# A long convolution and a two-matmul network: token tiles cut as groups of the last transform step, the first batch's last step put beside the network, and one engine for each first-step PSUM bank

## The chip, the cores and the metric

The kernel runs on one core of a Trainium2 chip. The metric is the device time of one execution in microseconds, as the median of several executions. A one-core program shows its executions within about 0.2% of each other here. The runs called fast lie within 1.5% of the fastest of the same kernel, and only such runs are compared, except for one single look that is marked.

Five units matter. **PE** is TensorE's matrix array and **PEld** its weight loads, **DVE** is VectorE, **ACT** is ScalarE, and **POOL** is GpSimd. DMA transfers are issued from a sixth queue.

## The reference, cut to what matters

```python
def _attn_ref(x, v, pos_emb, w1, w2):           # x, v: (4, 12480, 128)
    h_filt = (np.maximum(pos_emb @ w1, 0.0) @ w2) * np.exp(-0.01 * pos)[:, None]
    u = x * v
    y = irfft(rfft(u, n=2*S, axis=1) * rfft(h_filt, n=2*S, axis=0)[None], n=2*S, axis=1)[:, :S]
    return x * y

def _moe_ref(x, w_in, w_out):                   # x: (49920, 128), w_in 128x2048, w_out 2048x128
    h = x @ w_in
    return (h * np.cos(h)) @ w_out
```

The first part is a causal convolution along 12480 positions, for 4 batches of 128 channels. The second part is a network applied to each of the 49920 tokens. Everything is fp32.

## The kernel before

The convolution is a Fourier transform split as 96 by 120, so that each of its steps is a set of matmuls with small tables. There are four steps per batch: the **first step** (`f1`), the **middle step** with the product with the filter's spectrum (`f2`), the **third step** (`i1`) and the **last step** (`i2`). Between them the data lies in one SBUF array, `slots`. The last step works in 30 groups. A group yields 4 × 104 output rows of 128 channels, and needs four rows of tables (`tm`).

The network works on tiles of tokens, in 16 steps a tile. A step is: an up matmul into a hidden PSUM bank `ph`, ACT's `a`, DVE's `k`, GpSimd's `f` (range reduction), ACT's sine `cs`, DVE's gate `gt`, and a down matmul that adds to the accumulator `acc`:

```python
TOK = 4 * N2                                    # 480 tokens a tile, 26 tiles a batch
ps_acc = tile_pool(name="ps_acc", bufs=1, space=PSUM)    # accumulator
ps_h   = tile_pool(name="ps_h",  bufs=4, space=PSUM)     # hidden ring, also for transposes
ps_c   = tile_pool(name="ps_c",  bufs=3, space=PSUM)     # banks "cv" of the transforms
# one pass of the loop is one step:
    hidden[i] = moe_up(mpool, n, c)                       # PE up, ACT a, DVE k, POOL f
    gates[i - 1] = moe_act(mpool, *hidden.pop(i - 1))     # ACT cs, DVE gt
    if i >= LAG:                                          # LAG = 4
        pn, pc = steps[i - LAG]
        moe_down(pn, pc, gates.pop(i - LAG))              # PE down
        if pc == NFC - 1:
            ots[pn] = moe_evict(mpool, pn)                # ACT copies acc to ot
    ...                                                   # transposes of the next and last tile
    owed += 1.0
    while owed > 0.0:
        owed -= next(conv, owed)                          # a piece of a transform
```

The generator `conv` yields pieces of the transforms of later batches, each with a weight in network steps. Before, only the transforms of batches 1 to 3 ran beside the network. Batch 0 was finished first, with its last step as a stage of its own:

```python
with tc.tile_pool(name="spare", bufs=2) as pool:
    for _ in i2_units(bank, 0, 3, lambda t, n2: make_third(pool, t, n2, bank)):
        pass
...
def convolutions():
    here = NT * NFC - 3 * NFC
    less = here / (CONV_STEPS + H // UA * U_STEPS)
    for steps in u_units(1, 4, slots[0:R, :, :, :], nc.vector):   # load x and v of batch 1
        yield steps * less
    for b in range(1, B):
        for steps in conv_units(bank, b):       # b == 1 makes all table rows once more, stores them
            yield steps * (less if b == 1 else 1.0)
        ready = b
```

A first-step bank was emptied by two engines in turn, as the filter's version shows (the data's version has one copy on ACT and two instructions on DVE):

```python
def f1_evict_filter(ps, b):
    ...
    nc.scalar.copy(out=fnear[0:ODD, :, :, b, :], in_=near[0:ODD])
    nc.vector.tensor_copy(out=fnear[ODD:KE, 0, :, b, :], in_=near[ODD:KE, 1])
    nc.scalar.copy(out=ffar[0:ODD, :, :, b, :], in_=far[0:ODD])
    nc.scalar.copy(out=ffar[ODD:KE, 0, :, b, :], in_=far[ODD:KE, 1])
    yield
    nc.vector.tensor_scalar(out=fnear[ODD:KE, 1, :, b, :], in0=near[ODD:KE, 0], scalar1=-1.0, ...)
    nc.scalar.activation(ffar[ODD:KE, 1, :, b, :], far[ODD:KE, 0], AF.Copy, scale=-1.0)
    yield
```

Of the kernel before, what the change touches and what calls it, by code (L numbers as in the profile page):

```python
# [16 lines left out]
P = 128  # L17
# [13 lines left out]
def kernel(  # L31
# [43 lines left out]

    nc = tc.nc
# [23 lines left out]
    TOK = 4 * N2  # L100
# [7 lines left out]
    zd = dram.tile([B, R, N2, D], F32, name="zd")  # L108
# [3 lines left out]
    woutd = dram.tile([P, NFC, D], F32, name="woutd")  # L112
# [11 lines left out]
    def to_float32(pool, dst, raw):  # L124
# [21 lines left out]
        nc.gpsimd.tensor_tensor(low[:, :], high[:, :], power[:, :].bitcast(F32), op=ALU.mult)  # L146
        nc.sync.dma_start(dst, low[:, :])
# [3 lines left out]
    weights = []  # L151
    for c in range(0, DFF, WCOL):
        weights.append((wind[:, c:c + WCOL], in_words[:, c:c + WCOL, :]))
    for c in range(0, NFC, WCOL // D):
        weights.append((woutd[:, c:c + WCOL // D, :],
                        out_words[:, c:c + WCOL // D, :, :]))
# [13 lines left out]
    class Tables:  # L170
        def __init__(self, pool):
            self.pool = pool
            self.prod, self.moved, self.turned = (
                pool.tile([P, P], F32, name=name) for name in ("prod", "moved", "turned"))
# [8 lines left out]
        def sines(self, row, column, turn, outs, eighths=None):  # L183
# [4 lines left out]
            nc.vector.tensor_scalar(out=base, in0=row[0:p, 0:n],  # L188
                                    scalar1=column[0:p, 0:1], scalar2=None, op0=ALU.mult)
            if eighths is not None:  # L190
                nc.vector.tensor_scalar(out=base[:, eighths], in0=base[:, eighths],
                                        scalar1=float(turn // 8), scalar2=None, op0=ALU.add)
            for dst, quarters in outs:
# [3 lines left out]
                nc.vector.tensor_scalar(out=m, in0=base, scalar1=quarters,  # L197
                                        scalar2=None, op0=ALU.add)

                nc.vector.tensor_scalar(out=t, in0=m, scalar1=1.0 / turn, scalar2=ROUND,  # L200
                                        op0=ALU.mult, op1=ALU.add)
                nc.vector.tensor_scalar(out=t, in0=t, scalar1=ROUND, scalar2=float(turn),
                                        op0=ALU.subtract, op1=ALU.mult)
                nc.vector.tensor_tensor(t, m, t, op=ALU.subtract)
                nc.scalar.activation(dst, t, AF.Sin, scale=TWO_PI / turn)

    def forward_tables(pool):
        t = Tables(pool)
# [22 lines left out]
    def inverse_tables(pool):  # L231
        t = Tables(pool)
# [40 lines left out]

    def make_third(pool, t, n2, half=None):

        if n2 % 3 < 2:
            make_t(t, n2, half=half)
        else:
            spare = pool.tile([N1, 2, R], F32, name="spare")
            make_t(t, n2, spare=spare[:, :, :])  # L280
# [103 lines left out]
    def f1_evict_filter(ps, b):  # L384
        pj = ps[:, 0:4 * N1].rearrange("p (i r k) -> p r k i", i=2, r=2)
        near, far = pj[:, :, 0:KF], pj[:, :, KF:N1]
        nc.scalar.copy(out=fnear[0:ODD, :, :, b, :], in_=near[0:ODD])
        nc.vector.tensor_copy(out=fnear[ODD:KE, 0, :, b, :], in_=near[ODD:KE, 1])
        nc.scalar.copy(out=ffar[0:ODD, :, :, b, :], in_=far[0:ODD])
        nc.scalar.copy(out=ffar[ODD:KE, 0, :, b, :], in_=far[ODD:KE, 1])  # L390
        yield
        nc.vector.tensor_scalar(out=fnear[ODD:KE, 1, :, b, :], in0=near[ODD:KE, 0],
                                scalar1=-1.0, scalar2=None, op0=ALU.mult)
        nc.scalar.activation(ffar[ODD:KE, 1, :, b, :], far[ODD:KE, 0], AF.Copy, scale=-1.0)
        yield

    def f1_evict(ps, b):
        pj = ps[:, 0:4 * N1].rearrange("p (i r k) -> p r k i", i=2, r=2)
        nc.scalar.copy(out=parts[0:ODD, :, :, b, :], in_=pj[0:ODD])
        nc.vector.tensor_copy(out=parts[ODD:KE, 0, :, b, :], in_=pj[ODD:KE, 1])  # L400
        yield
        nc.vector.tensor_scalar(out=parts[ODD:KE, 1, :, b, :], in0=pj[ODD:KE, 0],
                                scalar1=-1.0, scalar2=None, op0=ALU.mult)
        yield
# [51 lines left out]
    def i2_out(pool, ps, xs, b, g):  # L456
# [4 lines left out]
        for h in range(2):  # L461
            n2 = n2s(g)[h * UA]
# [152 lines left out]
    def conv_units(bank, b):  # L615
# [12 lines left out]
        for _ in keep:  # L628
            pass
# [272 lines left out]
```

## Time and profile before

| | before |
|---|---|
| median of the runs, us | 4011.0 (4009.4 to 4016.2) |
| span of the profiled run, us | 4013.5 |
| filter's first step, us | 94 to 200 |
| batch 0: first, middle, third step, us | 200–288, 288–393, 393–464 |
| batch 0's last step, alone, us | 464–548 |
| network's first matmul, us | 550 |
| nothing but the network from, us | 3001 |

The forty slices of the kernel before, of PE's busy time and of the clock that was granted to it, in tenths, 100 us to a digit:

```profile
PE   5879878999999999999999999999999999999999
PEclk7579998999999999999999999999999999999999
```

From the eighth slice on PE is at 90% or more. What can be gained lies in the first seven slices, or in PE's own work. The **loss** of a stretch is its length less the time that its matmul records need at the record spacing seen where PE runs dense: 402.5 ns for a network record of 480 columns, 162.7 for the first step, 217 for the middle step, 102.5 for the third, 111 for the last, about 100 for a transpose. Edges of stretches are whole microseconds, so a sum over three batches is good to about 3 us. No matmul record of the network or of the mixed transforms is missing from the traces of before (6656 of the network), so none counts as loss by mistake.

Two more lines of before are needed later. They are groups from DVE's groups by shape in the load stretch 550 to 688 us: product of x and v, and `k`. Columns are busy time, mean ns of one, and idle time before them:

```profile
L368 DVE TENSOR_TENSOR xt<-xt,vt 104x256 f32<-104x256 f32 x60 | 59.7, 1011 | 0.0
L673 DVE TENSOR_SCALAR k<-a 128x480 f32<-128x480 f32 x56 | 23.0, 411 | 12.0 <-ACT a L670 11.9
```

The product takes 59.7 of the 131 us that DVE is busy there.

### The profile page before, as it was taken

To read this page: it belongs to the slowest core of one execution; us is meant where nothing else is said; L and a number is where in the kernel's file an instruction comes from. 1 tells how busy PE (TensorE), PEld (TensorE's weight loads), DVE (VectorE), ACT (ScalarE), POOL (GpSimd) and SP (SyncE) were. 2 spreads that over 40 slices of the span, in tenths; PEclk is the share of its full clock that TensorE was granted. 3 is DMA by queue.
4 is the path that set the end of the run, shared out by engine and by line. 5 is a ranking of instruction groups with operands and counts; after the bars stand their busy time and mean duration, and the time that the engine had idled before them with its cause. 6 is when DMAs were issued, how large, how long until landed. Compare 5 with 4: busy or idle time off the path is not lost.

```text
span 4013.5 us, 49256 instructions
## 1 busy us (share of the span) xinstructions
PE 3811.5 (95%) x13882; PEld 2227.9 (56%) x13882; DVE 2870.6 (72%) x6111; ACT 2589.5 (65%) x4905; POOL 2654.6 (66%) x2490
## 2 busy tenths in 40 slices
PE   5879878999999999999999999999999999999999
PEld 4666743655565655555656565556664444444444
DVE  3368669988887877887668777876556666666666
ACT  3544545866675566666655576665547777777777
POOL 6136657788865655887456658884447777777776
PEclk7579998999999999999999999999999999999999
DMA  4015353123216601221046202220350000000000
GB/s 131 26 49 175 93 140 86 53 81 85 70 49 178 190 24 35 78 74 49 11 138 173 82 26 63 78 69 15 86 159 19 20 20 20 15 20 20 20 15 15
DMA packets 285244, 276.12 MB, mean 69 GB/s; under 512 B 17389, under 2 KB 247885, under 8 KB 284717
## 3 DMA queue, kind: packets, MB, share of 16 engines
q1 hardware_dynamic: 284973, 272.99, 24.5%
q8 instruction: 111, 1.82, 0.2%
q14 instruction: 160, 1.31, 0.1%
HBM read 192.61 MB, written 80.31 MB: 68 GB/s over the span
## 4 chain that ended last, share of the span: by engine, by line
PE 75%; POOL 5%; DVE 3%; ACT 2%; DMA 2%; issue 2%; SPq 0%; POOLq 0%; DVEq 0%; ACTq 0%
PE ph L667 30%; PE acc L691 24%; PE cv L691 6%; PE cv L453 4%; PE cv L428 4%; POOL f L676 3%; PE cv L380 3%; PE cv L410 3%; PE ph L121 2%; ACT cs L681 1%; DVE k L673 1%; DMA zd<-zs 1%; DVE xt L368 1%; POOL slots L423 1%; DVE gt L683 1%
## 5 line engine op out<-in xcount | busy, mean ns | idle before, releaser
L676 POOL TENSOR_TENSOR f<-a,k 128x480 f32<-128x480 f32 x1664 | 2006.0, 1206 | 1030.2 <-DVE k L673 1001.7
L667 PE MATMUL ph<-at,w_in_sb 128*128 128x480 f32 x3328 | 1627.7, 571 | 21.0 <-DVE gt L683 20.1
L670 ACT ACTIVATE a<-ph,quarter 128x480 f32<-128x480 f32 x1664 | 1100.0, 661 | 711.4 <-PE ph L667 663.8
L683 DVE TENSOR_TENSOR gt<-ph,cs 128x480 f32<-128x480 f32 x1664 | 1092.2, 656 | 349.2 <-ACT cs L681 333.2
L691 PE MATMUL acc<-gt,w_out_sb 128*128 128x480 f32 x2720 | 1326.1, 569 | 8.7 <-ACT ot L696 8.1
L681 ACT ACTIVATE cs<-f 128x480 f32<-128x480 f32 x1664 | 998.8, 600 | 403.6 <-POOL f L676 401.5
L673 DVE TENSOR_SCALAR k<-a 128x480 f32<-128x480 f32 x1664 | 798.4, 480 | 548.1 <-ACT a L670 531.4
L691 PEld LDWEIGHTS acc<-gt,w_out_sb 128*128 128x128 f32 x2720 | 515.0, 190 | 603.6 <-issue 567.2
L667 PEld LDWEIGHTS ph<-at,w_in_sb 128*128 128x128 f32 x3328 | 593.6, 191 | 384.3 <-issue 286.0
L423 POOL TENSOR_TENSOR slots<-slots,t 120x256 f32<-120x256 f32 x384 | 307.2, 806 | 72.2 <-PE ps L410 36.8
L691 PE MATMUL cv<-gt,w_out_sb 128*128 128x480 f32 x608 | 294.2, 566 | 0.5 <-DVE gt L683 0.5
L453 PEld LDWEIGHTS cv<-slots,tm 96*104 96x104 f32 x1440 | 178.8, 169 | 78.1 <-issue 66.9
L428 PEld LDWEIGHTS cv<-cs,slots 120*96 120x96 f32 x1536 | 178.2, 167 | 71.5 <-issue 62.1
L453 PE MATMUL cv<-slots,tm 96*104 96x128 f32 x1440 | 189.2, 273 | 11.6 <-DMA tm<-td 7.9
L428 PE MATMUL cv<-cs,slots 120*96 120x120 f32 x1536 | 186.2, 267 | 6.0 <-POOL slots L423 6.0
L691 PEld LDWEIGHTS cv<-gt,w_out_sb 128*128 128x128 f32 x608 | 115.4, 190 | 130.3 <-issue 128.3
L380 PEld LDWEIGHTS cv<-c,slots 104*124 104x124 f32 x768 | 135.0, 195 | 82.9 <-issue 58.3
L410 PE MATMUL cv<-slots,w 124*120 124x256 f32 x576 | 173.3, 381 | 5.2 <-DMA h<-hd 4.6
L380 PE MATMUL cv<-c,slots 104*124 104x192 f32 x768 | 156.7, 331 | 17.3 <-POOL slots L356 15.3
L410 PEld LDWEIGHTS cv<-slots,w 124*120 124x120 f32 x576 | 103.2, 184 | 115.7 <-issue 102.7
L438 DVE TENSOR_TENSOR slots<-cv,other 96x240 f32<-96x240 f32 x384 | 136.3, 394 | 4.3 <-ACT other L436 4.3
L374 POOL TENSOR_TENSOR slots<-xt 104x256 f32<-104x256 f32 x120 | 117.4, 978 | 31.8 <-PE ph L667 17.8
(116 smaller groups left out, 2940.0 us busy)
## 6 DMA issues: line engine op xcount, KB each, us to landing
h<-hd SPq DMA_DIRECT2D x144, 240.0 KB
tm<-td SPq DMA_DIRECT2D x90, 312.0 KB
xt<-in_x_dram SPq DMA_DIRECT2D x120, 208.0 KB
vt<-in_v_dram SPq DMA_DIRECT2D x120, 208.0 KB
xs<-in_x_dram SPq DMA_DIRECT2D x120, 208.0 KB
zd<-zs SPq DMA_DIRECT2D x240, 104.0 KB
zb<-zd SPq DMA_DIRECT2D x104, 240.0 KB
out_dram<-ob SPq DMA_DIRECT2D x104, 240.0 KB
```

The costliest lines, as they stand in the source:

```text
L380: nc.tensor.matmul(ps[0:KE, i * 2 * N1:(i + 1) * 2 * N1], u[:, b, 0:KE, i], c1[0:u.shape[0], :, :].rearrange("p r k -> p (r k)"), start=Tr ...
L410: nc.tensor.matmul(ps[0:N2, i * 2 * D:(i + 1) * 2 * D], w[:, i, :], src[0:KE], start=True, stop=True)
L423: nc.gpsimd.tensor_tensor(y[:, r], y[:, r], t[:, r], op=op)
L428: nc.tensor.matmul(ps[0:N1, (i * 2 + r) * N2:(i * 2 + r + 1) * N2], parts[0:N2, r, :, b, i], cs[:, r, :], start=True, stop=True)
L453: nc.tensor.matmul(ps[0:R, i * D:(i + 1) * D], t[:, i, r, :], slots[0:N1, :, place, :], start=(r == 0), stop=(r == 1))
L667: nc.tensor.matmul(ph[:, 0:TOK], w_in_sb[:, c * P:(c + 1) * P], ats[n][:, :], start=True, stop=True)
L670: nc.scalar.activation(a[:, :], ph[:, 0:TOK], AF.Identity, bias=quarter[:, 0:1], scale=INV_TWO_PI)
L673: nc.vector.tensor_scalar(out=k[:, :], in0=a[:, :], scalar1=ROUND, scalar2=ROUND, op0=ALU.add, op1=ALU.subtract)
L676: nc.gpsimd.tensor_tensor(f[:, :], a[:, :], k[:, :], op=ALU.subtract)
L681: nc.scalar.activation(cs[:, :], f[:, :], AF.Sin, scale=TWO_PI)
L683: nc.vector.tensor_tensor(gt[:, :], ph[:, 0:TOK], cs[:, :], op=ALU.mult)
L691: nc.tensor.matmul(accs[n][:, 0:TOK], w_out_sb[:, c, :], gt[:, :], start=(c == 0), stop=(c == NFC - 1))
```

## The change

The intent is to start the network earlier. If a tile of the network is exactly one group of the last step (4 × 104 = 416 tokens), the network can begin when the first group of batch 0 is there. The other 27 or so groups, their table rows and the loads of batch 1 then lie beside network steps. A second, independent part lets one engine empty a whole first-step bank (ACT the even ones, DVE the odd ones). Smaller parts: the tables of the inverse steps are made on GpSimd, and `w_out` is converted straight into SBUF. The diff, cut to its core:

```diff
-    TOK = 4 * N2
+    TOK = G * R                                  # 4 * 104; 30 tiles a batch
-    zd = dram.tile([B, R, N2, D], F32, name="zd")
+    zd = dram.tile([B, N2 // G, R, G, D], F32, name="zd")
@@ inverse_tables
-        t = Tables(pool)
+        t = Tables(pool, nc.gpsimd)
@@ first step
+    def f1_takers(b):
+        if b % 2 == 0:
+            return nc.scalar.copy, lambda out, in_: nc.scalar.activation(
+                out, in_, AF.Copy, scale=-1.0)
+        return nc.vector.tensor_copy, lambda out, in_: nc.vector.tensor_scalar(
+            out=out, in0=in_, scalar1=-1.0, scalar2=None, op0=ALU.mult)
+    def f1_evict(ps, b, places=None):
+        copy, negated = f1_takers(b)
+        pj = ps[:, 0:4 * N1].rearrange("p (i r k) -> p r k i", i=2, r=2)
+        for dst, k in places or ((parts, slice(0, N1)),):
+            copy(out=dst[0:ODD, :, :, b, :], in_=pj[0:ODD, :, k])
+        yield
+        for dst, k in places or ((parts, slice(0, N1)),):
+            copy(out=dst[ODD:KE, 0, :, b, :], in_=pj[ODD:KE, 1, k])
+            negated(dst[ODD:KE, 1, :, b, :], pj[ODD:KE, 0, k])
+        yield
@@ weights of the pieces, in network steps
-    U_STEPS, F1_STEPS, F2_STEPS, I1_STEPS, I2_STEPS = 2.2, 0.9, 3.1, 0.9, 1.6
-    I2U_STEPS = 3.4
+    U_STEPS, F1_STEPS, F2_STEPS, I1_STEPS, I2_STEPS = 2.5, 1.0, 3.5, 1.0, 1.8
+    FIRST_STEPS, I2U_STEPS = 4.4, 3.8
@@ last step: batch 0 makes its table rows (three by ACT and DVE, one by ACT and GpSimd) and stores them
+                if b == 0:
+                    for i in range(G):
+                        if i < G - 1:
+                            make_t(ts[j][:, i, :, :], n2s(j)[i])
+                        else:
+                            spare = pool.tile([N1, 2, R], F32, name="spare", bufs=1)
+                            make_t(ts[j][:, i, :, :], n2s(j)[i], spare=spare[:, :, :])
+                    nc.sync.dma_start(td[j, :, :, :, :], ts[j][:, :, :, :])
+                else:
                     nc.sync.dma_start(ts[j][:, :, :, :], td[j, :, :, :, :])
...
-        for h in range(2):
-            n2 = n2s(g)[h * UA]
-            nc.sync.dma_start(zd[b, :, n2:n2 + UA, :], zs[:, h, :, :])
+        nc.sync.dma_start(zd[b, g, :, :, :], zs[:, :, :, :].rearrange("p h n d -> p (h n) d"))
+        made[0] += 1
@@ order
-            with tc.tile_pool(name="spare", bufs=2) as pool:
-                for _ in i2_units(bank, 0, 3, lambda t, n2: make_third(pool, t, n2, bank)):
-                    pass
...
+            for b in range(B):
+                yield from inverse_units(bank, b)       # last step of b, loads of b + 1
+                if b + 1 < B:
+                    yield from forward_units(bank)      # first, middle, third step of b + 1
...
-            while ready < n // NT:
+            while made[0] <= n:
                 next(conv)
```

## The prediction

> **What bounds the kernel now.** I read the forty slices first, then busy time by stretch (edges placed where each group of instructions first and last appears), then the waits of the evicting instructions, then the timeline. The stretches, in us, each engine's busy time with its instruction count, then granted clock, DMA share and GB/s:
>
> ```profile
> 94.00:200.00 106.00, 94.21 (x257) 67.94 (x258) 39.83 (x125) 58.86 (x229) 22.43 (x37) 0.55 0.12 34
> 200.00:288.00 88.00, 63.13 (x256) 57.07 (x255) 57.74 (x213) 41.24 (x120) 30.74 (x32) 0.72 0.13 37
> ...
> 464.00:548.00 84.00, 61.06 (x480) 57.49 (x480) 47.98 (x110) 44.07 (x117) 56.16 (x80) 0.91 0.60 170
> 548.00:688.00 140.00, 109.80 (x244) 44.42 (x244) 130.84 (x202) 69.87 (x122) 100.16 (x87) 0.91 0.37 103
> ...
> 3003.00:3980.00 977.00, 977.00 (x2643) 474.04 (x2642) 641.59 (x1177) 773.33 (x1285) 708.17 (x588) 1.00 0.07 19
> ```
>
> The order is PE, PEld, DVE, ACT, POOL. From 3003 us on only the second part (the two-matmul network) runs and PE is full: there matmul columns are the bound. Four early stretches are not PE-bound: the first transform step of the filter (94 to 200), the same step of batch 0 (200 to 288), the last step of batch 0 alone (464 to 548), and the loading of batch 1 beside the network (548 to 688), where DVE is busy 131 of 140 us.
>
> The filter's first step is a ping-pong. The groups' idle time before them, and what ended it:
>
> ```profile
> L388 DVE COPY ftile<-ps 60x144 f32<-60x144 f32 x64 | 19.9, 311 | 44.6 <-ACT ftile L387 44.6
> L389 ACT COPY slots<-ps 64x96 f32<-64x96 f32 x64 | 14.9, 233 | 24.2 <-DVE ftile L388 24.2
> L392 DVE TENSOR_SCALAR ftile<-ps 60x144 f32<-60x144 f32 x64 | 19.9, 311 | 28.2 <-ACT slots L390 27.8
> L394 ACT ACTIVATE slots<-ps 60x48 f32<-60x48 f32 x64 | 13.2, 206 | 24.2 <-DVE ftile L392 24.2
> ```
>
> ACT, DVE, ACT, DVE, ACT empty one PSUM bank in turn, each waiting for the other. In the timeline this repeats every 1.81 us for each of 64 banks, although neither engine works over 1.03 us per bank. PE waits for banks, at half clock (0.55).
>
> Two matmul lines of the pure tail give the unit of PE work:
>
> ```profile
> 3302.18 0.97 PE L667 MATMUL ph<-at,w_in_sb 128*128 128x480 f32 x2
> 3302.98 0.97 PE L691 MATMUL cv<-gt,w_out_sb 128*128 128x480 f32 x2
> ```
>
> One fp32 matmul is two records, 0.805 us start to start, or 402.5 ns a record of 480 columns. A step (up and down) is 1.61 us, a 16-step tile 25.76, plus about 0.8 for eight transposes: 26.55 us. (2643 records in 977 us, 72 a tile, gives 26.6.)
>
> **What the Trainium skill says.** "TensorE: Matmul & The Clock Gate", section "Wait — 56ns, not 53.3ns?", gives start to start N/2.4 GHz plus a fixed 2.5 ns when warm. Here a record takes two cycles a column plus the same 2.5 (480/1.2+2.5=402.5), so a narrower tile costs almost nothing per column. The same page, "What's actually happening", says that the clock is throttled by default and released by activity; the 0.55 in the ping-pong and 1.00 in the tail agree. "PSUM — Partial Sum Buffer", section "Terms", says that two engines in one bank and quadrant at once is an error; the trace shows the order kept by waits, 64 times 0.7 us on DVE alone. "GPSIMD Engine Reference", section "1. Specifications", says that GpSimd shares its SBUF interfaces with VectorE, with contention when DVE reads two SBUF inputs. The product of x and v on DVE agrees: 1030 ns each between 560 and 680 us beside a busy GpSimd, 678 ns each between 1220 and 1400.
>
> **The change part by part.**
>
> *One engine a bank.* Even banks go to ACT, odd ones to DVE; the built order shows that the cross-engine waits are gone. Back-to-back instructions overlap by about 0.09 us in the timeline. With one duration plus slope per engine from the rows above, six evictions of a filter bank take about 1.05 us on ACT or 1.22 on DVE, so two banks per 1.22. PE needs 4 records of 192 columns, 0.65 us a bank warm, 1.3 a pair. So PE-bound and dense: the clock should be released, 64 × 0.65 = 42 us, plus some 8 for eight load groups of batch 0 that share DVE and GpSimd. 106 becomes 50: **55 us gained**. In batch 0's own step a pair costs DVE about 1.0 instead of 2 × 0.55, little different, and the eight weight conversions still stall DVE 2.3 us each. The sine tables move from DVE (an 11 us stall) to GpSimd, whose 96x208 tensor_scalar takes 846 ns: some 40 small instructions, 20 to 35 us, partly beside the DVE banks and ended later by ACT's in-order queue. I take +3 us net. Batch 0's end of the third step moves from 464 to **412**.
>
> *No stage of its own for batch 0's last step.* The network's first tile needs one group of the last step, not a whole batch. In the built order three groups are issued before the first tile is loaded back: table rows, matmul, product, store (about 3 us), load (about 3 us), transpose, and a table buffer that waits for its own store. I estimate 18 us from 412: the network starts at **430** instead of 550, with 27 groups still to do.
>
> *PE work after that.* Tiles are 4 × 104 = 416 columns: 349.2 ns a record by the rule above, 64 × 0.3492 + 0.8 = 23.15 us, × 120 tiles = 2778 us (before 26.55 × 104 = 2761). Transforms by record spacing in the timeline: last step 480 × 0.111 = 53.4, third 512 × 0.1025 = 52.5, first 256 × 0.163 = 41.6, second 192 × 0.217 = 41.6 us a batch. After: 4 × 53.4 − 5 for the three early groups, + 3 × (52.5 + 41.6 + 41.6) = 616. Together **3394 us**.
>
> *What PE loses.* Check on before: 550 + 2761 + 3 × 189.1 = 3878, + 9 of tail; 4013 leaves about 127. The load stretch loses 50 (244 records, 54 steps of 1.66 = 90 of 140 us); the ten mixed stretches of three batches lose about 77 by the same count, and 0 in the tail. After: mixed stretches about **65**, since batch 1 no longer computes table rows and the network is spread wider (I count 581 of 1920 steps left for the pure tail). The new first stretch has for each of 30 groups 4.4 steps, a group of the last step, four table rows and a load group. PE: 4.4 × 1.447 + 1.78 = 8.15 us. DVE: 8.8 network instructions of about 0.53, two products of 0.68 to 1.03, a sum 0.43 to 0.76, zs 0.68, three table rows of 0.57: 9.2 less 16 overlaps of 0.08, so about 8. POOL about 7.4, ACT 6.2. Three engines near 8 us in fixed order will not interleave perfectly: 1 us a group, **30 us**. Shorter steps leave less slack for the four-bank ring of hidden tiles (chain from up to gate about 4.3 us against 4 × 1.4 less one bank during transposes) and for the single accumulator: **8 us**. End: **9 us**.
>
> Sum: 430 + 3394 + 65 + 30 + 8 + 9 = **3936 us**, 1.9% under 4011.
>
> **The rivals.** (1) *DVE takes the place of the removed stage.* The first stretch is then a stretched load stage; DVE was 93% busy there before, and now has table rows too. At 10.5 us a group it loses 70, not 30, and the time is about 3975. For it: the 1030 ns products. Against: the step counts give more network work per group than the 1.8 steps of before. (2) *416 columns expose ACT or GpSimd.* GpSimd's 1206 ns at 480 becomes about 1.05 at 416 against a step of 1.40, ACT's pair about 1.0; both fit, but if the ring of four banks stalls 0.5 us a tile, 60 us go and the time is near 3995. (3) *The gains are larger*: the mixed stretches lose 45 and the first stretch 10, as DVE has one PSUM instruction fewer per pair of banks; 3895. (4) *DMA hides anyway.* Rows of zd and out grow to 2 KB and 1 KB runs, but loads were hidden (12 us of PE waits in all), so fewer, longer packets change nothing outside the start.
>
> **Range and chances.** The early gain is the surest term (55, give or take 12), the first stretch and the ring of banks the least (each give or take 25). Together about 35 us of spread: 3936, 8 in 10 between 3885 and 3985. Two per cent is 3931, almost the centre: faster 0.46, same 0.52, slower 0.02.
>
> **What would show it.** Right: filter step near 50 us at clock near 1; network's first matmul near 430; PE start to start 349 ns in the tail, a tile near 23.2 us; DVE and PE both near 90% in the first stretch of some 270 us. Wrong: the filter step still at half clock; tables holding ACT over 30 us; PE gaps behind gate products or f in the tail; a first stretch over 300 us.

## The result, and the profile after

| | before | after |
|---|---|---|
| median, us | 4010.2 (4 runs, 4008.8 to 4016.2) | 3969.2 (4 runs, 3967.8 to 3971.8) |
| ratio to before | | 0.9896, 95% interval 0.9879 to 0.9913 |
| filter's first step, us | 106 | 46 |
| batch 0: first, middle, third step, us | 88, 105, 71 | 88, 105, 69 |
| network's first matmul, us | 550 | 421 |
| nothing but the network from, us | 3001 | 3092 |
| tile of the pure network, us | 26.6 | 23.35 |

A ratio here is the mean time of one kernel's fast runs over the mean of the other's fast runs of the same rounds, so it is not quite the ratio of the medians. The change gains 1.0%: inside two per cent, and inside the predicted range, 33 us above the predicted centre.

The forty slices of the changed kernel, PE and clock:

```profile
PE   5788898999999999999999999999999999999999
PEclk8999999999999999999999999999999999999999
```

The clock is now 0.8 in the first slice and 0.9 or more from the second on. Busy time by stretch of the changed kernel follows. The order is PE, PEld, DVE, ACT, POOL, then clock, DMA share and GB/s. The stretches are the filter's first step, batch 0's first step, batch 0's third step, the first stretch of the network, one middle step beside the network, and the pure network:

```profile
94.00:140.00 46.00, 44.78 (x255) 42.89 (x256) 42.34 (x169) 37.16 (x187) 26.20 (x43) 0.96 0.26 76
140.00:228.00 88.00, 53.82 (x260) 43.08 (x259) 53.66 (x157) 43.98 (x134) 47.00 (x71) 0.90 0.11 37
333.00:402.00 69.00, 55.83 (x511) 54.27 (x510) 46.73 (x152) 28.03 (x81) 31.71 (x34) 0.98 0.15 47
421.00:696.00 275.00, 244.96 (x983) 146.90 (x981) 238.85 (x446) 174.88 (x375) 211.12 (x208) 0.97 0.44 130
1672.00:1972.00 300.00, 293.20 (x956) 170.19 (x956) 238.39 (x532) 198.64 (x371) 251.57 (x264) 1.00 0.24 71
3092.00:3960.00 868.00, 867.53 (x2670) 474.66 (x2668) 595.54 (x1188) 688.14 (x1297) 634.98 (x594) 1.00 0.06 19
```

The filter's first step has nearly the same PE records as before in 46 us instead of 106, at a clock of 0.96 instead of 0.55. The groups of its evictions in the changed kernel answer to the four ping-pong lines of before:

```profile
L389 ACT COPY ftile<-ps 64x288 f32<-64x288 f32 x32 | 12.6, 393 | 10.7 <-PE ps L373 4.7 <-DMA xt<-in_x_dram 3.8
L389 DVE COPY ftile<-ps 64x288 f32<-64x288 f32 x27 | 12.2, 450 | 2.8 <-PE ps L373 2.0
```

ACT no longer waits for DVE, nor DVE for ACT: what ends their idle time is PE or a load. Two lines of the timeline of the pure network in the changed kernel give the unit of its work:

```profile
3300.34 0.86 PE L643 MATMUL ph<-at,w_in_sb 128*128 128x416 f32 x2
3301.04 0.86 PE L667 MATMUL cv<-gt,w_out_sb 128*128 128x416 f32 x2
```

They start 0.70 us apart, so a record takes about 349 ns, as predicted.

Where the time went is seen by adding up the losses of all stretches. Each column names what ran beside the network; "first" is the load stretch of before or the first stretch of after.

| us | start | first | f1 | f2 | i1 | i2 | pure network |
|---|---|---|---|---|---|---|---|
| before | 550 | 48.7 | 18.9 | 20.3 | 17.8 | 19.4 | 2.6 |
| after | 421 | 48.4 | 10.0 | 43.2 | 14.3 | 22.0 | 8.5 |

With 3393 us of matmul records after the start and 6 us at the end, the column of after adds up to 421 + 3393 + 48.4 + 89.5 + 8.5 + 6 = 3966, which is the span of its profiled run. Two numbers stand out. The first stretch lost 48 us although its network steps are dense, and the middle step's loss more than doubled. For the first stretch, DVE's groups by shape:

```profile
L649 DVE TENSOR_SCALAR k<-a 128x416 f32<-128x416 f32 x126 | 86.7, 688 | 8.2 <-ACT a L646 7.9
L255 DVE SCALAR_TENSOR_TENSOR tm<-rows,tw_t,tm 96x208 f32<-96x208 f32 x77 | 35.0, 504 | 1.6 <-ACT tm L253 1.6
L361 DVE TENSOR_TENSOR xt<-xt,vt 104x256 f32<-104x256 f32 x60 | 32.1, 537 | 0.0
```

Here `k` of 416 columns takes 688 ns, where `k` of 480 columns took 411 in the load stretch of before, and the product that took 1011 ns takes 537. Such means move with what GpSimd is doing, as sorting the single instructions of the traces shows (a count over all of them). In batch 1's middle step of the changed kernel, 836 to 1141 us, the 46 `k` that started while GpSimd was idle took 368 ns (median). The 110 that took over 470 ns had all started while a GpSimd instruction was running, and ended 232 ns (median) after it. In the first stretch the 35 that started clear of GpSimd took 364 ns, and all 53 over 470 ns had started beside a running GpSimd instruction; so had, in the load stretch of before, all 48 of the 60 products that took over 510 ns (the other 12 took 413). So here `k` and the product wait for a GpSimd instruction that is under way. The gate `gt` did not: 577 ns clear of GpSimd and 592 beside it.

For the middle step, PE's own waits (us in total, times, longest), first in the changed kernel at 1672 to 1972 us:

```profile
PE acc L667 <- ACT ot L672: 5.5, 10, 0.9
PE ph L643 <- DVE gt L659: 0.4, 2, 0.2
```

And in the kernel before, in its corresponding stretch from 1570 to 1868 us:

```profile
PE cv L410 <- DMA h<-hd: 4.6, 1, 4.6
PE acc L691 <- ACT ot L696: 1.7, 5, 0.6
```

In the changed kernel PE waits once at every tile boundary, for the copy that empties the only accumulator. In batch 1's middle step (836 to 1141 us) it waits 6.0 us for this copy, and another 4.8 us for hidden banks `ph` that the gates still hold. One such boundary, PE first:

```profile
1807.04 0.86 PE L667 MATMUL acc<-gt,w_out_sb 128*128 128x416 f32 x2
1807.73 0.52 PE L122 MATMUL ph<-ident,zb 104*128 104x104 f32 x4
1808.09 0.61 PE L403 MATMUL cv<-slots,w 124*120 124x256 f32 x2
1808.54 0.92 PE L643 MATMUL ph<-at,w_in_sb 128*128 128x416 f32 x2
1810.32 0.96 PE L667 MATMUL acc<-gt,w_out_sb 128*128 128x416 f32 x2 [0.86 <-ACT ot L672]
```

ACT at the same time, in the changed kernel:

```profile
1807.72 0.59 ACT L646 ACTIVATE a<-ph,quarter 128x416 f32<-128x416 f32 x1
1809.32 0.55 ACT L657 ACTIVATE cs<-f 128x416 f32<-128x416 f32 x1 [1.01 <-POOL f L652]
1809.78 0.49 ACT L672 COPY ot<-acc 128x416 f32<-128x416 f32 x1
```

The last matmul into the accumulator started at 1807.04 and was done by about 1807.9. ACT stood idle for 1.01 us until 1809.32, waiting for GpSimd's `f`, because the sine `cs` is ahead of the copy `ot` in its queue. The next tile's first down matmul came about 1.1 us late (1810.32 instead of 1809.24, two records after 1808.54). "TensorE: Matmul & The Clock Gate", section "Architectural detail: the array is 16× 32×32, not 1× 128×128", says that the queues of ACT and DVE are strict FIFO; this is that rule at work, with 1.01 us of idle ACT beside it.

GpSimd's own durations shrink less than the tiles do. The group of `f` in the pure network (3100 to 3500 us) of the changed kernel:

```profile
L652 POOL TENSOR_TENSOR f<-a,k 128x416 f32<-128x416 f32 x275 | 294.3, 1070 | 107.8 <-DVE k L649 107.8
```

And of the kernel before:

```profile
L676 POOL TENSOR_TENSOR f<-a,k 128x480 f32<-128x480 f32 x241 | 290.6, 1206 | 110.3 <-DVE k L673 110.3
```

It took 1206 ns at 480 columns and takes 1070 at 416, so 2.125 ns a column and 186 ns that do not shrink. "GPSIMD Engine Reference", section "3.1 Elementwise — side-by-side cycle accounting", gives about 2.6 cycles an element for a two-input operation; at the 1.2 GHz of its section 1, 2.125 ns is 2.55 cycles, so page and trace agree.

This does not yet say why the copy comes too late in one kernel and not in the other. The busy times of the kernel before, in its corresponding middle step, are:

```profile
1570.00:1868.00 298.00, 295.25 (x864) 155.29 (x864) 236.32 (x489) 196.49 (x326) 253.72 (x243) 0.99 0.26 73
```

GpSimd is busy 254 of 298 us there and 252 of 300 in the changed kernel, DVE 236 and 238, ACT 196 and 199. No engine has more to do; what differs is that a step leaves 1.40 us of matmul time instead of 1.61 for its chain of instructions. That this is the cause is likely, but no run isolates it.

### The profile page after: what moved, and what is told of

It is laid out like the page before. It is cut to its first block, busy times and chain, and to the rows that moved or that the text cites. A ratio compares the mean times of both kernels' runs of the same rounds, so it can differ in the third digit from the quotient of the medians.

```text
span 3966.0 us, 52667 instructions
## 1 busy us (share of the span) xinstructions
PE 3773.5 (95%) x15034; PEld 2382.9 (60%) x15034; DVE 2903.8 (73%) x6443; ACT 2611.8 (66%) x5409; POOL 2654.3 (67%) x2692
## 4 chain that ended last, share of the span: by engine, by line
PE 65%; POOL 11%; DVE 8%; ACT 6%; issue 3%; DMA 2%; SPq 0%; POOLq 0%; DVEq 0%; ACTq 0%
PE ph L643 25%; PE acc L667 20%; POOL f L652 7%; PE cv L667 5%; PE cv L446 4%; PE cv L421 4%; ACT cs L657 3%; PE cv L373 3%; POOL slots L416 3%; DVE gt L659 2%; PE ph L122 2%; DVE k L649 2%; DVE t L415 1%; DMA hd<-h 1%; PE cv L403 1%
## 5 line engine op out<-in xcount | busy, mean ns | idle before, releaser
L652 POOL TENSOR_TENSOR f<-a,k 128x416 f32<-128x416 f32 x1920 | 2053.7, 1070 | 1036.6 <-DVE k L649 1033.2
L643 PE MATMUL ph<-at,w_in_sb 128*128 128x416 f32 x3840 | 1675.0, 518 | 28.1 <-DVE gt L659 27.4
L646 ACT ACTIVATE a<-ph,quarter 128x416 f32<-128x416 f32 x1920 | 1160.2, 604 | 538.0 <-PE ph L643 528.7
L657 ACT ACTIVATE cs<-f 128x416 f32<-128x416 f32 x1920 | 1051.2, 548 | 573.7 <-POOL f L652 571.2
L659 DVE TENSOR_TENSOR gt<-ph,cs 128x416 f32<-128x416 f32 x1920 | 1134.3, 591 | 402.5 <-ACT cs L657 394.7
L667 PE MATMUL acc<-gt,w_out_sb 128*128 128x416 f32 x3232 | 1404.3, 516 | 22.1 <-ACT ot L672 21.7
L649 DVE TENSOR_SCALAR k<-a 128x416 f32<-128x416 f32 x1920 | 913.7, 476 | 500.7 <-ACT a L646 467.0
L667 PEld LDWEIGHTS acc<-gt,w_out_sb 128*128 128x128 f32 x3232 | 609.8, 190 | 559.5 <-issue 500.3
L643 PEld LDWEIGHTS ph<-at,w_in_sb 128*128 128x128 f32 x3840 | 677.1, 190 | 361.3 <-issue 222.7
L667 PE MATMUL cv<-gt,w_out_sb 128*128 128x416 f32 x608 | 261.7, 513 | 0.5 <-DVE gt L659 0.4
```

What stands on the lines that cost most here:

```text
L643: nc.tensor.matmul(ph[:, 0:TOK], w_in_sb[:, c * P:(c + 1) * P], ats[n][:, :], start=True, stop=True)
L646: nc.scalar.activation(a[:, :], ph[:, 0:TOK], AF.Identity, bias=quarter[:, 0:1], scale=INV_TWO_PI)
L649: nc.vector.tensor_scalar(out=k[:, :], in0=a[:, :], scalar1=ROUND, scalar2=ROUND, op0=ALU.add, op1=ALU.subtract)
L652: nc.gpsimd.tensor_tensor(f[:, :], a[:, :], k[:, :], op=ALU.subtract)
L657: nc.scalar.activation(cs[:, :], f[:, :], AF.Sin, scale=TWO_PI)
L659: nc.vector.tensor_tensor(gt[:, :], ph[:, 0:TOK], cs[:, :], op=ALU.mult)
```

## The experiments

Twelve kernels ran (the record has no e6). Each is told with its edit against the kernel that it starts from. Ratios are to the kernel before of the same rounds. The losses of all of them, in the form of the table above:

| us | median | ratio | start | first | f1 | f2 | i1 | i2 | pure network |
|---|---|---|---|---|---|---|---|---|---|
| e1: before + one engine a bank | 3957.1 | 0.9863 | 486 | 47.7 | 24.3 | 20.9 | 14.7 | 22.4 | 3.6 |
| e2: after, two engines a bank | 4039.0 | 1.0066 | 488 | 44.3 | 8.7 | 43.5 | 15.3 | 24.0 | 14.5 |
| e4: before + tiles of 416 | 4068.8 | 1.0140 | 549 | 47.8 | 20.2 | 53.3 | 12.4 | 25.0 | 10.2 |
| e5: e1 + tiles of 416 | 4011.8 | 0.9991 | 490 | 48.7 | 20.9 | 52.6 | 14.7 | 22.6 | 10.2 |
| e3: after, transposes in `cv` banks | 3997.3 | 0.9962 | 423 | 49.6 | 21.1 | 51.6 | 25.3 | 22.0 | 5.8 |
| e7: after, F2_STEPS 4.0 | 3974.1 | 0.9899 | 424 | 46.4 | 10.0 | 45.3 | 20.1 | 19.8 | 7.4 |
| e8: after, one sum on DVE | 3963.6 | 0.9872 | 422 | 45.5 | 10.7 | 39.4 | 12.3 | 24.7 | 8.3 |
| e9: after, FIRST_STEPS 5.4 | 3978.6 | 0.9911 | 425 | 47.5 | 9.7 | 45.8 | 15.5 | 20.0 | 13.6 |
| e12: after, rows not made | 3943.6 | (one run) | 425 | 20.5 | 9.7 | 43.2 | 14.3 | 22.0 | 8.5 |
| e11: after, early `ot` | 3957.7 | 0.9860 | 423 | 44.4 | 7.7 | 37.2 | 18.3 | 24.5 | 1.5 |
| e13: e11 and e8 | 3946.3 | 0.9836 | 421 | 43.2 | 9.7 | 32.2 | 14.3 | 22.0 | 1.8 |
| e10: e1, load stretch spread | 3951.4 | 0.9846 | 490 | 43.8 | 20.3 | 18.4 | 17.3 | 21.9 | 2.8 |

### What each part of the change is worth: e1, e2, e4, e5

**e1** is the kernel before with `f1_evict` and `f1_evict_filter` of the change, and nothing else of it.

> The kernel before with the one-engine emptying of first-step banks alone; tiles, stages and tables as before. Theory A (the emptying carries the whole gain, the new tiles and the early start of the second part cancel or cost): the filter's first step falls from 106 to about 46 us, batch 0's own step from 88 to about 84, and the three mixed first steps lose 9 us instead of 19, so about 4010-60-4-10 = 3936 us, faster than the changed kernel's 3969. Rival B (all parts help, the intended early start too): the emptying is only a part of the 41 us, so the time lies between 3969 and 4010.

It took 3957.1 us, 0.9863 (0.9849 to 0.9878). The stretches of e1, the filter's first step and the load stretch:

```profile
94.00:141.00 47.00, 45.40 (x254) 43.63 (x255) 42.47 (x171) 36.94 (x187) 23.77 (x37) 0.94 0.26 77
486.00:623.00 137.00, 108.64 (x240) 43.97 (x240) 130.47 (x202) 69.34 (x121) 100.11 (x87) 0.92 0.36 105
```

The filter's step fell to 47 us, batch 0's own first step from 88 to 85 (141 to 226 us), and the network started at 486 instead of 550. After that the loss of every stretch is that of before within the error, except in the mixed first steps: the further gain that was expected there did not come, and they lost 24.3 us against 18.9. This single part alone beats the whole change, 3957 against 3969, though narrowly: the intervals of the two ratios just fail to meet (up to 0.9878, from 0.9879).

**e2** is the reverse: the changed kernel with the two eviction functions of before.

> The changed kernel with the old two-engine emptying put back, all else kept. Theory A: 3969+70 = about 4040 us, slower than before (4010), with the filter's first step back at 106 us and half clock. Rival B: between 3969 and 4010, since the early start still pays.

It took 4039.0 us, 1.0066 (1.0051 to 1.0081). The network started at 488 instead of 421. Without the one-engine emptying, the rest of the change is a loss of 0.7%.

**e4** is the kernel before with tiles of 416 tokens and the step weights scaled to match, with batch 0's last step still alone.

```diff
-    TOK = 4 * N2
+    TOK = 4 * R
...                                              # loads, transposes and stores in rows of R, not N2
-    U_STEPS, F1_STEPS, F2_STEPS, I1_STEPS, I2_STEPS = 2.2, 0.9, 3.1, 0.9, 1.6
-    I2U_STEPS = 3.4
+    U_STEPS, F1_STEPS, F2_STEPS, I1_STEPS, I2_STEPS = 2.5, 1.0, 3.5, 1.0, 1.8
+    I2U_STEPS = 3.8
```

> The kernel before with tiles of 416 rows instead of 480 (four blocks of 104 consecutive rows, a whole batch still needed first), and the step weights of the changed kernel. If narrower tiles cost only what the prediction said (17 us of columns and transposes, 8 of slack): about 4035 us. If, as the count of the changed kernel's stretches suggests, the middle step of the transform (f2) loses 40 us instead of 22 and the pure tail 7 instead of 1: 4010+17+19+6+3 = about 4055 us. The pure tail should show 23.3 to 23.4 us a tile.

It took 4068.8 us, 1.0140 (1.0125 to 1.0156). The tile's width, with the weights that go with it, brought the middle step's loss from 20 to 53 us, so the early start of the change is not what causes it. (That it is not the weights either is seen in e7 below, where another half step a unit left the loss alone.) Of PE's waits, 6.0 us were for hidden banks and 5.9 for the accumulator in one middle step, 1603 to 1903 us. The pure network's loss went from 2.6 to 10.2.

**e5** has both: e1 with tiles of 416, and still the late start. So it is the changed kernel without the early start and the smaller parts.

> The kernel before with one-engine emptying and 416-row tiles, but still a whole batch before the second part starts: the changed kernel without its early start. If the three parts add up: 4069 (416 rows alone) less 55 to 60 = about 4011 us, so that the early start is worth 4011-3969 = about 40 us. If they interact, as the mixed first steps of the changed kernel hint (loss 9 instead of 20 us): about 4000.

It took 4011.8 us, 0.9991 (0.9976 to 1.0006): the narrow tiles give back all that the one-engine emptying won.

Worked out from differences of these ratios, times 4012 us: one engine a bank gains 55 us on the kernel before (e1), and 68 on the rest of the change (e2 to after). Tiles of 416 cost 56 us alone (e4) and 51 beside one engine (e1 to e5). The early start with its smaller parts gains 38 us (e5 to after) or 30 (e4 to e2). Both ways round add up: −55 + 51 − 38 = −42, and +56 − 30 − 68 = −42. The cost of the tiles splits by the loss table of e4 into 17 us of PE work (2778 against 2761, the prediction's count), 35 us in the mixed stretches (110.9 against 76.4) and 8 us in the pure network, together 60 for 56 measured.

### What the first stretch loses: e9 and e12

**e9** is the changed kernel with one more network step a group of the first stretch.

```diff
-    FIRST_STEPS, I2U_STEPS = 4.4, 3.8
+    FIRST_STEPS, I2U_STEPS = 5.4, 3.8
...
-                    yield from forward_units(bank)
+                    for steps in forward_units(bank):
+                        yield steps * (0.9 if b == 0 else 1.0)
```

> The changed kernel with 5.4 instead of 4.4 network steps per group of the first stretch, and 0.9 of the steps in the first forward transform so that batch 1 is not later. If busy VectorE and its order set the first stretch (loss 48 us): 30 more steps of 1.45 us of PE work cost only 25 to 30 us there, the loss falls to about 32, the denser forward transform gives back 3 to 5: about 3957. If each step itself carries the loss: the stretch grows by 30 x 1.8 = 54 us and the time stays at 3969 or rises.

It took 3978.6 us, 0.9911. The first stretch grew from 275 to 315 us with 28 more steps, and each of those steps cost its 1.43 us of PE work; the loss stayed at 47.5. More matmuls do not fill the gaps, so the loss belongs to the groups, about 1.6 us each. The time still rose by 9 us: the start came 4 us later, and the pure network lost 13.6 us instead of 8.5.

**e12** gives a wrong result. Batch 0's table rows are loaded from another array that already lies in DRAM, instead of being made.

```diff
-                    for i in range(G):
-                        if i < G - 1:
-                            make_t(...)
-                        else: ...  make_t(..., spare=spare[:, :, :])
+                    start = hd[0, 0, 0, 0, 0:1]
+                    nc.sync.dma_start(ts[j][:, :, :, :], bass.AP(tensor=start.tensor,
+                        offset=start.offset + j * N1 * G * 2 * R, ap=[[G * 2 * R, N1], [1, G * 2 * R]]))
```

> Wrong result on purpose: the changed kernel, with batch 0's table rows loaded from an unrelated array already in DRAM instead of made, so the first stretch keeps its steps, products, loads and stores but loses three table rows on DVE and ACT and one on GpSimd a group. Theory A (DVE's table rows, beside the load products, carry the first stretch's loss; before, the load stretch lost 49 us with no rows but with only 1.8 steps a group): first-stretch loss falls from 48 to about 20 us, the time to about 3940 us. Theory B (rows are hidden; the loss per group comes from the products of x and v and the sums that share DVE and GpSimd with the network): loss stays above 38 us, time about 3962.

It was one look, so its state is unknown; but its later stretches lose what those of the changed kernel lose to within 0.4 us. It took 3943.6 us. The first stretch of e12, and its `k`:

```profile
425.00:672.00 247.00, 232.87 (x982) 146.01 (x981) 193.53 (x368) 146.96 (x273) 164.70 (x157) 0.98 0.63 182
```

```profile
L647 DVE TENSOR_SCALAR k<-a 128x416 f32<-128x416 f32 x126 | 69.0, 548 | 23.7 <-ACT a L644 18.6 <-POOL f L650 2.2 <-POOL slots L367 0.6
```

The loss fell from 48.4 to 20.5 us, as theory A said. DVE's busy time fell by 45 us, GpSimd's by 46 and ACT's by 28. Of DVE's 45, 18 are `k` alone, which went from 688 to 548 ns. In this stretch PE's waits for hidden banks fell from 19.9 us to 0.6, while 7.3 us of waits for the loaded rows came in, which the changed kernel does not have there. So the table rows carry at least 28 of the 48 us, through their own time and through what they do to the instructions beside them. Which of the three engines' rows it is was not told apart.

### What the middle step loses: e3, e7, e8, e11, e13

**e3** moves the transposes of the network out of the ring of hidden banks into the banks of the transforms (`pt = bank()` in two places of the changed kernel).

> The changed kernel with the tiles' transposes in the transforms' PSUM banks, so that the four hidden banks hold hidden tiles only. If the ring of four hidden banks is what shorter steps run into: the pure tail goes from 23.35 to 23.15 us a tile (7 us), and the middle step's loss from 41 to about 30, so about 3950 us. If the middle step is held by busy VectorE and GpSimd instead: the tail gains 5 us, the mixed stretches gain nothing or lose by a bank fewer for the transforms, 3960 to 3985 us.

It took 3997.3 us, 0.9962. The pure network's loss fell from 8.5 to 5.8, but the mixed stretches lost 30 us more (120.0 against 89.5). The three transform banks have nothing to give away.

**e7** gives the middle step more network steps (`F2_STEPS` 3.5 to 4.0 in the changed kernel).

> The changed kernel with 4.0 instead of 3.5 network steps per unit of the middle transform step. If GpSimd's queue (f of the network between two products of the transform) sets the pace there, more network per product thins it out: the loss of the three middle stretches falls from 41 to about 25 us although they hold 72 steps more, 3955 us or a little more, since batch 1's first group is now late by some 20 steps. If the loss belongs to the network's tile edges (accumulator and transposes), it grows with the steps: 41 to 47 us, about 3975.

It took 3974.1 us, 0.9899. With 72 more network steps in it, the middle step lost 45.3 us. So the loss is not thinned out, and more time for the same transform work does not help. Time and loss are those that were expected if the loss belongs to the tile edges (3975, 41 to 47 us); but the rise of 2 us is inside the error, so that the loss grows with the steps is not shown.

**e8** moves one of the two sums of each middle-step unit from GpSimd to DVE, beside the network only.

```diff
-            nc.gpsimd.tensor_tensor(y[:, r], y[:, r], t[:, r], op=op)
+            sums[r].tensor_tensor(y[:, r], y[:, r], t[:, r], op=op)   # sums = (nc.gpsimd, nc.vector)
```

> The changed kernel with one of the two sums of each mixed middle-step unit on VectorE instead of GpSimd: GpSimd sheds 48 x 0.8 = 38 us a batch of 252, VectorE gains 48 x 0.42 = 20 of 240. If GpSimd sets the pace: the loss of the middle stretches falls from 41 to 20-25 us, about 3950. If VectorE is as tight: no gain, 3969 or more. The pure tail and first stretch stay.

It took 3963.6 us, 0.9872. GpSimd's busy time in a middle step fell from 252 to 216 us and the loss from 43.2 to 39.4. The interval of the ratio, 0.9855 to 0.9888, overlaps that of the changed kernel, and 3.8 us is hardly more than the error; that the same edit took another 5.0 us off the loss in e13 below speaks for it. GpSimd's load has a part in it, but a small one. In PE's waits of e8 in the middle stretch the accumulator is still there at every tile boundary:

```profile
PE acc L668 <- ACT ot L673: 4.2, 10, 0.7
```

This line, and the pattern in the timeline shown above, led to **e11**: at the last step of a tile, the copy of the accumulator is put ahead of the sine in ACT's queue.

```diff
+            ends = i >= LAG and steps[i - LAG][1] == NFC - 1
-            if 0 <= i - 1 < len(steps):
+            if not ends and 0 <= i - 1 < len(steps):
                 gates[i - 1] = moe_act(mpool, *hidden.pop(i - 1))
             if i >= LAG:
                 ...
                 if pc == NFC - 1:
                     ots[pn] = moe_evict(mpool, pn)
+            if ends and 0 <= i - 1 < len(steps):
+                gates[i - 1] = moe_act(mpool, *hidden.pop(i - 1))
```

> The changed kernel with one pair of ACT instructions swapped per tile: at a tile's last step the copy that empties the accumulator (ot) stands ahead of that step's sine (cs), not behind it. In the middle-step stretch 1672 to 1972 of the changed kernel, 8.1 of 9.4 us of gaps over 0.3 us between matmul records stand between an up and a down matmul and end with ot, about 0.8 us a tile (before: 3.3 us in all); ACT idles there about 1 us on a sine that waits for GpSimd's f, with ot behind it. Theory A (the added loss of the middle step is this queue order, exposed because a 416-column step leaves the ot copy less matmul time to hide in): the wait of the accumulator for ot goes to nearly 0, the middle steps' loss falls from 43 to 22 us in three batches, first stretch 48 to about 43, time about 3942 us, ratio about 0.983. Theory B (GpSimd and DVE cannot keep up with the narrower steps; the accumulator only shows where the lost time surfaces): the gaps move to hidden banks waiting for gates; middle-step loss stays above 36 us, time 3960 to 3970.

It took 3957.7 us, 0.9860 (0.9846 to 0.9875). ACT of e11 at the same tile boundary:

```profile
1806.46 0.59 ACT L646 ACTIVATE a<-ph,quarter 128x416 f32<-128x416 f32 x1
1806.95 0.49 ACT L672 COPY ot<-acc 128x416 f32<-128x416 f32 x1
1808.07 0.55 ACT L657 ACTIVATE cs<-f 128x416 f32<-128x416 f32 x1 [0.63 <-POOL f L652]
```

The copy now fills the idle time before the sine. PE's waits of e11 in this stretch:

```profile
PE ph L643 <- DVE gt L659: 3.1, 8, 0.5
PE cv L421 <- POOL slots L416: 1.6, 2, 1.2
```

The accumulator's wait is gone from the list, so that part of theory A is shown. But the middle step's loss fell only to 37.2, and not to 22, since a new wait came: hidden banks for gates, 3.1 us. Over the three middle steps PE's waits for the accumulator went from 16.9 us to none, and those for hidden banks rose from 5.8 to 14.7. The third and last steps lost 6.5 us more, of which the error can be half. Theory B's bound on the loss (above 36) held and its mechanism was seen, and both theories missed more than half of the gain: 7 us of 12 came in the pure network (8.5 to 1.5). There the transposes of a finished tile and the matmul after them each took 0.1 us longer than dense in the changed kernel (0.535 against 0.435 us for four transposes), and no longer do so in e11. Why they were slow was not found out.

**e13** has e11 and e8 together, in five rounds.

> The changed kernel with both partial cures of the middle step at once: the accumulator copied out ahead of the sine (alone: middle-step loss 43 to 37 us, what was left moved to up matmuls that wait for gates, about 5 us a stage) and one of the two sums of the mixed middle step on DVE (alone: 43 to 39, the accumulator's waits of 6.5 us a stage unchanged). Theory A (two causes, each of which hides the other's cure: GpSimd's late f delays the gates and the queue order delays the accumulator): together middle-step loss falls to 22 to 28 us, time about 3943 us, ratio about 0.982. Theory B (the sums only add: 43 less 6 less 4): loss 32 to 35 us, time 3951 to 3954.

It took 3946.3 us, 0.9836 (0.9822 to 0.9849). The middle step's loss of 32.2 us is in the range that theory B gave: the two cures add up, and neither hides the other. In time, too, they add: the ratios of e11 and e8 lie 0.0036 and 0.0024 under that of the changed kernel, and e13's lies 0.0060 under it. Theory B's time of 3951 to 3954 was set too high for that. The three middle steps tell different things, though. The second one is as good as in the kernel before (6.2 us lost against 7.6), and nothing is left of the waits at the accumulator. The first one, batch 1's, still loses 15.8. PE's waits of e13 there, from 831 to 1134 us:

```profile
PE ph L644 <- DVE gt L660: 7.9, 12, 1.1
```

These are up matmuls, most of them right after transposes, that wait for a hidden bank. One difference is in the trace: `k` took 542 ns in batch 1's middle step, and 477 and 508 in those of batches 2 and 3, while `f` took 1069 to 1071 in all three. Of about 169 `k` in each, 94, 66 and 68 took over 470 ns, and every one of these had started beside a running GpSimd instruction. But in the kernel before `k` (of 480 columns) took 600 ns in batch 1's middle step, and only about 7 us were lost there, so a long `k` alone is not the cause. Why batch 1's middle step suffers from this and batch 2's does not was not found out.

### A spread load stretch on the better start: e10

**e10** is e1 with 2.8 network steps for a load group, where the weights gave about 1.8; batch 1's later steps get fewer.

> The kernel before with the one-engine emptying (it ran at 3957 us), and its load stretch spread: 2.8 network steps a load group, where the weights now give about 1.8, so that the stages of batch 1 that follow get fewer steps each. Theory A (the load stretch loses because too few matmul columns stand beside each load group): its loss falls from 48 to about 25 us, the later stretches lose 5 more, time about 3940 us, ratio about 0.982. Theory B (the loss belongs to the load group, as in the changed kernel, where 28 more steps in the first stretch left its loss at 47.5): loss stays 45 to 50 us, time 3955 to 3962.

It took 3951.4 us, 0.9846 (0.983 to 0.9862). With 30 more steps the load stretch lost 43.8 us instead of 47.7, so this loss, too, belongs mostly to the group. Loss and time lie between the ranges of the two theories, nearer to B's. The time is 6 us under e1's, with intervals that overlap. Both the changed and the unchanged kernel are beaten by e1, e10, e11 and e13. The best median is e13's, but its interval overlaps those of e10 and e11.

## Why the prediction was right or wrong

The direction, the verdict of within 2% and the range held. The 33 us above the centre are 43 us of loss that were not foreseen, less 12 us by which start and end came out better, and 3 us between span and median; so the range held in part because errors cancelled. The terms, and what they measured in the changed kernel:

| term, us | predicted | measured |
|---|---|---|
| filter's first step | 50 | 46 |
| end of batch 0's third step | 412 | 402 |
| network's first matmul | 430 | 421 |
| PE work after that | 3394 | 3393 |
| first stretch, loss | 30 | 48 |
| mixed stretches, loss | 65 | 90 |
| ring and accumulator (pure network), loss | 8 | 8.5 |
| end | 9 | 6 |
| sum | 3936 | 3966 (span), 3969 (median) |

- **One engine a bank: right.** The ping-pong was the cause of the half clock. The step went to 46 us at a clock of 0.96. e1 measured the 55 us that were predicted for this part alone, but so exact a fit is luck: the filter's step gave 59 us (106 to 47), batch 0's own step 3, and the mixed stretches gave some 6 back (82.3 us lost against 76.4).
- **The tables on GpSimd** were counted as +3 us, and cost about that. Batch 0's first step stayed at 88 us because two effects cancel: with one engine a bank and the tables on VectorE it took 85 us (e1 and e5), in the changed kernel 88. With two engines a bank it took 88 us without and 95 with the tables on GpSimd (e4, e2).
- **The early start: right in kind.** It came at 421, mostly because the three terms before it were each a little better. With its cost in the first stretch it is worth 30 to 38 us (e5 to after, e4 to e2).
- **The count of PE work: right** to 1 us, with the rule of two cycles a column and 2.5 ns. (What is measured here is the number of records times their spacing, 349 ns at 416 columns in the trace.)
- **The first stretch: mis-sized.** The step that failed is "Three engines near 8 us in fixed order will not interleave perfectly: 1 us a group, **30 us**". The busy times behind it were right: DVE 239/30 = 8.0 us a group, POOL 7.0 for 7.4, ACT 5.8 for 6.2. So it was not an engine's load that was misjudged, but the loss of interleaving: 1.6 us a group instead of 1. e12 gives at least 28 of the 48 us to the table rows, and e9 shows that more steps do not dilute it. Rival 1, that DVE takes the place of the removed stage, expected 70 us and 3975; the truth lies between.
- **The mixed stretches: mis-sized, and this is the larger error.** The step that failed is "After: mixed stretches about **65**, since batch 1 no longer computes table rows and the network is spread wider". That effect exists: the first step's loss fell from 18.9 to 10.0, and in e4 and e5, where batch 1 still makes the rows, it is 20.2 and 20.9. But the tile's width was charged only to PE work (17 us) and to a term of 8 us, "Shorter steps leave less slack for the four-bank ring of hidden tiles [...] and for the single accumulator". e4 and e5 measured 51 to 56 us for the width, and most of it lies in the middle step, where the loss went from 20 to 43. The prediction named the accumulator, and gave it and the ring 8 us together. That the pure network alone lost 8.5 is luck: nothing in the prediction confines the 8 us to that stretch, where the accumulators of even and odd tiles are two. Beside transforms there is only one.
- **Rival 2**, that 416 columns expose ACT or GpSimd, came nearest: somewhat over half its size was measured (34 to 39 us of loss for 60). But the ring of hidden banks, which it named, is not where most of it showed. In the pure network PE's waits come to 0.4 us. In the three middle steps PE waited 16.9 us for the accumulator and 5.8 for hidden banks; a late `f` of GpSimd holds up ACT's queue there, and with it the accumulator, and only when that was cured (e11) did the ring's share grow. Relieving GpSimd by 36 us a middle step (e8) took off 4 us.
- **Rival 4**, that transfers are hidden anyway, agrees with what was seen: after the start PE waits for transfers 7.3 us in all in the changed kernel (table rows `tm`, in the last step), and 12.5 us in the kernel before (7.9 for `tm`, 4.6 for `h`).

What is shown: the split of the gain in three parts, the table rows' share of the first stretch, the accumulator's wait behind the sine and its cure, and, less firmly, a small share of GpSimd's sums. What stays open: why narrower tiles expose these waits although no engine has more to do, 12 us of the middle step's added 23 us that remain in e13, almost all of it in batches 1 and 3, why e11 gains 7 us in the pure network, and the 20 us that the first stretch loses without making table rows (7.3 of them are waits for e12's own loads).

## What to carry to other kernels

Charge a change of tile width to every per-tile and per-step hand-over beside the busiest other work, not only to the matmul columns: tiles narrower by 13% cost 17 us in matmul work and another 34 to 39 us of loss between matmuls, more than the 30 to 38 us gained by the early start that they allowed. Look for what stands ahead of a bank's last reader in an in-order queue; moving one copy ahead of a sine that was waiting anyway gained about 12 us. Where the mean of an instruction moves from stretch to stretch, sort its single durations by what another engine was doing when it started. And try the parts of a change alone: here one of them was better than the whole.

## What the Trainium skill lacked or had wrong

- "TensorE: Matmul & The Clock Gate", section "Wait — 56ns, not 53.3ns?": it gives N/2.4 GHz and 2.5 ns a matmul, and no time for fp32, whose passes the skill counts elsewhere. Here an fp32 matmul is two records of 402.5 ns at 480 columns and 349 ns at 416, each two cycles a column and the 2.5 ns.
- The same page, section "Architectural detail: the array is 16× 32×32, not 1× 128×128": it says that ACT's queue is strict FIFO, and does not say what that costs. Here a PSUM copy behind a waiting sine left ACT idle for 1.01 us at a tile boundary, and PE 1.1 us late.
- "GPSIMD Engine Reference", section "1. Specifications": it names contention with DVE for SBUF, and not, in this place, which engine waits and how long. DVE's `k` took 688 ns in the first stretch, 548 without table rows, and 411 (with more columns) in the load stretch of before; the product of x and v took 1011 ns in the load stretch of before and 537 in the first stretch. Sorted by single instructions, a `k` that starts beside a running GpSimd instruction ended 232 ns after that instruction's end (110 of 110 that took over 470 ns, in batch 1's middle step). No run measured what GpSimd loses in turn.
- The same page, section "3.1 Elementwise — side-by-side cycle accounting": its 2.6 cycles an element agree with 2.55 here. It gives no figure in ns for the fixed cost of an instruction, which is 186 ns for `f`, worked out from 1206 and 1070 ns.
- "PSUM — Partial Sum Buffer", section "Terms": it has the rule for two engines in one bank, and nothing of what it costs to let two engines take turns at one. In the filter's first step of before DVE stood idle 0.7 us a bank until ACT was done, and 106 us became 46 (47 in e1) when one engine emptied the whole bank.
